# One core, attention fused with a rational-activation MLP: the iteration written as a table of 19 steps, one factor moved to another engine, sketches repeated by transfers

## The chip, the cores and the metric

The kernel runs on one core of a Trainium2 chip. The core has five engines that run their own queues of instructions in order and wait for each other on semaphores: PE (TensorE, matmuls; its weight loads are listed apart as PEld), DVE (VectorE), ACT (ScalarE), POOL (GpSimd) and SP (SyncE, which here only issues DMAs). The metric is the device time in microseconds. Three runs of the kernel before gave 311.78, 308.90 and 311.98 us, so the median is 311.78 us.

## The reference

Inputs are q, k and v of shape (4 batches, 4 heads, 1088 tokens, 32), two sketch matrices S1 and S2 of shape (8, 32), and the MLP's weights.

```python
def phi(x):                       # 64 features of a token
    a = einsum('rd,bhsd->bhsr', S1, x)
    b = einsum('rd,bhsd->bhsr', S2, x)
    return einsum('bhsi,bhsj->bhsij', a, b).reshape(..., 64)
q_p, k_p = phi(q), phi(k)
kv  = einsum('bhsf,bhsd->bhfd', k_p, v);  z = sum(k_p, axis=2)
x   = (q_p @ kv) / (q_p @ z + 1e-6)       # then 4352 tokens x 128
h   = x @ w_in                            # 4352 x 2048
P   = a[0] + a[1]*h + a[2]*h**2 + a[3]*h**3
Q   = 1 + |b[0]|*|h| + |b[1]|*h**2
out = (P / (Q + 1e-6)) @ w_out            # 4352 x 128
```

## The kernel before, in words

**The MLP, which is most of the work,** is cut into 34 units. Two units hold 256 tokens and half of the 2048 hidden columns each; the other 32 hold 512 tokens and a quarter of the hidden columns each. A unit's tile is always 128 x 2048 elements. Its steps are: `hidden` (PE, h = w_in·x in float32, in two halves), `evac` (ACT, copies each half from PSUM to the bf16 tile `hh`), `d_abs` (DVE, u = |h|), `d_w` (DVE, w = |b1|·u + |b0|), `d_y` (DVE, y = w·u), `a_ln` and `a_exp` (ACT, r = exp(-ln(1 + 1e-6 + y)) = 1/Q), `d_s` (DVE, s = h·r), `d_hs` (DVE, h·s), the linear factor p = a3·h + a2 (`d_p` on DVE in even units, `a_p` on ACT in odd units), `d_g` (DVE, g = p·hs), and `gather` (PE, which sums r, s and g against three scaled bf16 copies of w_out, w_out·a0, w_out·a1 and w_out, in four parts). `store` turns the finished block of outputs (DVE) and sends it out (SP).

**The attention** makes the columns of xT that `hidden` reads. Per batch, `Keys` (part 0 and part 1) has transposes (DVE), sketches (PE), copies of one sketch (ACT), features (DVE, the outer product), products with v (PE, over the whole sequence) and keep (ACT, writes the small matrix kvz). Per batch five blocks of `Queries` follow (four of 256 tokens and one of 64), each with transposes (DVE), sketches (PE), copies (ACT), features (DVE), products (PE), quotient (DVE: add 1e-6, reciprocal, multiply), back (PE transpose) and keep (ACT, into xT). In `Queries.sketches` a constant matrix `SAB` holds every sketch row eight times, so that four matmuls (two sketches for each of two pairs of heads, 64 rows deep, 128 columns out) write both factors of the outer product, already repeated, to PSUM. `copies` then brings one factor to SBUF in two ACT copies and `features` multiplies in two DVE instructions.

**What sets the order.** Nothing is reordered by a scheduler: each engine runs its instructions in the order in which the code is written. A loop runs over i from 0 to 37. Iteration i does evac and DVE's first three steps of unit i, `hidden` of unit i+1, `a_ln`, `a_exp` and `a_p` of unit i-1, `d_s`, `d_p`, `d_hs` and `d_g` of unit i-2, and `gather` of unit i-3. Between these steps the loop calls `gap()` five times; each call takes the attention stages that `plan` holds for that number of gap. A block of queries gets its eight stages in eight gaps one after another, beginning at gap 40·b - 31 + 7, 15, 22, 29 or 35. On DVE an iteration begins with `d_abs`, before `d_s` and `d_p`.

**The opening**, ahead of the loop, loads S1, S2, k and q of batch 0, w_in and w_out, and does the keys and the first two blocks of queries. `turn(n)` puts n matmuls on an idle tile between the steps (`TURNS = (12, 3, 0, 2, 2)`). The six scaled or plain copies of w_out (`w_part`) stand in gaps 4 to 9, that is in iterations 0 and 1.

**Buffers.** The pool `att` has three PSUM banks, `hps` two double banks for `hidden`, `ops` one bank for the output sum.

Of the kernel before, what the change touches and what calls it, by code (L numbers as in the profile page):

```python
# [18 lines left out]

@with_exitstack  # L20
def kernel(
# [149 lines left out]
    class Keys:  # L171
        def __init__(self, b, k_sb, v_sb, first=False):
            self.dst, self.k_sb, self.v_sb = kvz[b % 2], k_sb, v_sb
            self.take = wide if first else bank
# [13 lines left out]
        def sketches(self, part):  # L188
            t0, n = self.PARTS[part]
            ab = self.ab[part] = self.take()[:, 0:n * H * 2 * R].rearrange("p (t h s r) -> p t h s r", h=H, s=2, r=R)  # L190
            for t in range(t0, t0 + n):
# [1 line left out]
                nc.tensor.matmul(ab[:sl, t - t0].rearrange("p h s r -> p (h s r)"),
                                 lhsT=self.kT[:, t * 128:t * 128 + sl],
                                 rhs=S12.rearrange("p h s r -> p (h s r)"), start=True, stop=True)
# [4 lines left out]

        def copies(self, part):
            b_sk = self.b[part] = tmp.tile([128, 5, H, R], FP, name="b_sk")
            for ts, te, sl in self.spans(part):
                nc.scalar.copy(out=b_sk[:sl, ts:te], in_=self.ab[part][:sl, ts:te, :, 1, :])
# [34 lines left out]
    class Queries:  # L239
# [49 lines left out]

        def quotient(self):  # L290
            tl, T = self.tl, self.T
            nd = self.nd[:tl, 0:T * H * KW].rearrange("p (t h x) -> p (t h) x", t=T, h=H)
# [1 line left out]
            nc.vector.tensor_scalar(out=rec[:tl, :T * H], in0=nd[:, :, D], scalar1=1e-6, scalar2=None, op0=AX.add)
# [307 lines left out]
```

## Time and profile before

| | value |
|---|---|
| three runs, us | 311.78, 308.90, 311.98 |
| the profiled execution's own time | 310.26 us |
| its span | 308.5 us |
| mean granted TensorE clock | 0.977 |
| busy: PE, DVE, ACT | 284.8, 271.2, 244.4 us |
| share of the span: PE, DVE, ACT | 92%, 88%, 79% |
| DMA | 11.29 MB, 37 GB/s on the mean |

All positions below are microseconds from the start of the span. 1.76 us of the execution's own time lie outside the span. Four stages can be told apart: the opening (0 to 20.5, until the first `hidden`), the first four units (20.5 to 60.08, the last number being the start of unit 4's evac), the middle, in which batches 1 to 3 of the attention run between the units (60.08 to 245.84, the start of unit 27's evac), and the end without attention (245.84 to 308.5). The middle repeats itself: unit 4's evac starts at 60.08, unit 12's at 125.87, unit 20's at 191.66, so a round of eight units, with one batch of attention in it, takes 65.79 us. "A <- B" means that A waited for B, or, in the names of an instruction's tiles, that A is computed from B.

### The profile page before, as it was taken

To read this page: it belongs to the slowest core of one execution; us is meant where nothing else is said; L and a number is where in the kernel's file an instruction comes from. 1 tells how busy PE (TensorE), PEld (TensorE's weight loads), DVE (VectorE), ACT (ScalarE), POOL (GpSimd) and SP (SyncE) were. 2 spreads that over 40 slices of the span, in tenths; PEclk is the share of its full clock that TensorE was granted. 3 is DMA by queue.
4 is the path that set the end of the run, shared out by engine and by line. 5 is a ranking of instruction groups with operands and counts; after the bars stand their busy time and mean duration, and the time that the engine had idled before them with its cause. 6 is when DMAs were issued, how large, how long until landed. Compare 5 with 4: busy or idle time off the path is not lost.

```text
span 308.5 us, 3853 instructions
## 1 busy us (share of the span) xinstructions
PE 284.8 (92%) x1439; PEld 149.5 (48%) x1439; DVE 271.2 (88%) x383; ACT 244.4 (79%) x241; POOL 2.7 (1%) x22
## 2 busy tenths in 40 slices
PE   6999768999999999999999999999999998999392
PEld 2778445665455455545445554454454343434141
DVE  3526699899989999899999999899999999999992
ACT  1122858899888976898979778998889899999770
POOL 3000000000000000000000000000000000000000
PEclk9599979999999999999999999999999999999899
DMA  5990000002700200005500200010001000200102
GB/s 168 280 260 4 2 1 0 2 1 49 187 0 0 34 2 0 3 0 129 124 0 0 34 2 1 2 30 7 0 0 28 8 0 0 35 1 0 28 6 35
DMA packets 24626, 11.29 MB, mean 37 GB/s; under 512 B 20384, under 2 KB 22432, under 8 KB 24608
## 3 DMA queue, kind: packets, MB, share of 16 engines
q1 hardware_dynamic: 22976, 10.64, 14.5%
q10 hardware_dynamic: 1632, 0.41, 0.7%
q8 instruction: 11, 0.18, 0.2%
q14 instruction: 7, 0.06, 0.1%
HBM read 8.82 MB, written 2.23 MB: 36 GB/s over the span
## 4 chain that ended last, share of the span: by engine, by line
PE 46%; ACT 33%; DVE 15%; issue 3%; DMA 2%; SPq 0%; DVEq 0%; ACTq 0%
PE h_ps L337 21%; PE out_ps L408 10%; ACT r L376 9%; ACT p L368 8%; ACT hh L343 7%; ACT ln L372 6%; PE att_ps L260 4%; PE att_ps L226 3%; PE att_ps L286 3%; DVE hs L384 2%; DMA k_sb<-in_k_dram 2%; DVE s L380 2%; DVE g L388 2%; DVE y L356 1%; DVE w L352 1%
## 5 line engine op out<-in xcount | busy, mean ns | idle before, releaser
L337 PE MATMUL h_ps<-xT,w_in_sb 128*128 128x512 f32 (+1 forms) x288 | 130.6, 586 | 6.3 <-ACT hh L343 4.4
L337 PEld LDWEIGHTS h_ps<-xT,w_in_sb 128*128 128x128 f32 x288 | 51.7, 192 | 54.5 <-issue 38.7
L408 PEld LDWEIGHTS <-w_out 128*128 128x128 bf16 x420 | 40.5, 100 | 58.6 <-issue 26.6
L343 ACT CAST hh<-h_ps 128x1024 bf16<-128x1024 f32 x68 | 65.7, 1020 | 2.0 <-PE h_ps L337 2.0
L372 ACT ACTIVATE ln<-y 128x2048 f32<-128x2048 bf16 x34 | 65.6, 1930 | 1.9 <-DVE y L356 1.8
L376 ACT ACTIVATE r<-ln 128x2048 bf16<-128x2048 f32 x34 | 65.1, 1915 | 0.7
L408 PE MATMUL out_ps<-r,w_out 128*128 128x512 bf16 (+1 forms) x140 | 52.1, 372 | 5.3 <-DVE out_sb L419 5.3
L408 PE MATMUL out_ps<-g,w_out 128*128 128x512 bf16 (+1 forms) x140 | 52.1, 372 | 0.2 <-DVE g L388 0.2
L408 PE MATMUL out_ps<-s,w_out 128*128 128x512 bf16 (+1 forms) x140 | 52.0, 371 | 0.0
L388 DVE TENSOR_TENSOR g<-p,hs 128x2048 bf16<-128x2048 bf16 x34 | 41.2, 1213 | 0.2
L380 DVE TENSOR_TENSOR s<-hh,r 128x2048 bf16<-128x2048 bf16 x34 | 41.4, 1216 | 0.0
L356 DVE TENSOR_TENSOR y<-w,u 128x2048 bf16<-128x2048 bf16 x34 | 41.2, 1212 | 0.0
L384 DVE TENSOR_TENSOR hs<-hh,s 128x2048 bf16<-128x2048 bf16 x34 | 40.8, 1201 | 0.0
L368 ACT ACTIVATE p<-hh,a_sb 128x2048 bf16<-128x2048 bf16 x17 | 35.4, 2081 | 0.0
L347 DVE TENSOR_SCALAR u<-hh 128x2048 uint16<-128x2048 uint16 x34 | 23.3, 685 | 13.4 <-ACT hh L343 13.4
L352 DVE TENSOR_SCALAR w<-u,b_abs 128x2048 bf16<-128x2048 bf16 x34 | 27.4, 806 | 0.0
L286 PEld LDWEIGHTS att_ps<-kvz,q_pT 128*128 128x128 f32 (+1 forms) x144 | 18.0, 185 | 6.8 <-issue 3.3
L270 ACT COPY a_sk<-att_ps 128x256 f32<-128x256 f32 (+1 forms) x36 | 10.3, 342 | 10.9 <-PE att_ps L260 10.9
L260 PE MATMUL att_ps<-qT,SAB 64*128 64x256 f32 (+1 forms) x144 | 18.5, 376 | 0.0
L286 PE MATMUL att_ps<-kvz,q_pT 128*128 128x66 f32 (+1 forms) x144 | 18.1, 266 | 0.0
L308 ACT COPY xT<-att_ps 128x256 f32<-128x256 f32 (+1 forms) x20 | 6.8, 340 | 12.5 <-PE att_ps L303 12.5
L260 PEld LDWEIGHTS att_ps<-qT,SAB 64*128 64x128 f32 x144 | 11.7, 186 | 9.2 <-DVE u L347 4.5
(52 smaller groups left out, 160.8 us busy)
## 6 DMA issues: line engine op xcount, KB each, us to landing
k_sb<-in_k_dram SPq DMA_DIRECT2D x4, 544.0 KB, 4.8
v_sb<-in_v_dram SPq DMA_DIRECT2D x16, 128.0 KB, 5.2
q_sb<-in_q_dram SPq DMA_DIRECT2D x3, 544.0 KB, 6.3
out_dram<-out_sb SPq DMA_DIRECT2D x18, 64.0 KB, 2.0
w_in_sb<-in_moe_w_in_dram SPq DMA_DIRECT2D x4, 256.0 KB, 3.5
q_sb<-in_q_dram SPq DMA_DIRECT2D x1, 288.0 KB, 5.1
q_sb<-in_q_dram ACTq DMA_DIRECT2D x1, 256.0 KB, 3.2
out_dram<-out_sb SPq DMA_DIRECT2D x4, 56.0 KB, 1.9
```

The lines of the kernel that those rows point to most:

```text
L260: nc.tensor.matmul(self.sk[hp][:, i], lhsT=SAB[i][p, :], rhs=self.qT[p, :n], start=True, stop=True)
L286: nc.tensor.matmul(self.nd[:self.tl, o:o + 2 * KW], lhsT=self.q_p[:, c, t * self.tl:(t + 1) * self.tl], rhs=kvz[self.b % 2][:, c, :], star ...
L337: nc.tensor.matmul(t[:, x * tl:(x + 1) * tl], lhsT=w_in_sb[:, f * 128:(f + 1) * 128], rhs=xT[:, t0:t0 + tl], start=True, stop=True)
L343: nc.scalar.copy(out=live[i]["hh"][:, part * 1024:(part + 1) * 1024], in_=live[i]["h", part])
L356: nc.vector.tensor_mul(out=t, in0=live[i]["w"], in1=live[i]["u"])
L368: nc.scalar.activation(out=t, in_=live[i]["hh"], func=ACT.Identity, scale=a3, bias=a2)
L372: nc.scalar.activation(out=t, in_=live[i]["y"], func=ACT.Ln, bias=1.0 + 1e-6)
L376: nc.scalar.activation(out=t, in_=live[i]["ln"], func=ACT.Exp, scale=-1.0)
L380: nc.vector.tensor_mul(out=t, in0=live[i]["hh"], in1=live[i]["r"])
L384: nc.vector.tensor_mul(out=t, in0=live[i]["hh"], in1=live[i]["s"])
L388: nc.vector.tensor_mul(out=t, in0=live[i]["p"], in1=live[i]["hs"])
L408: nc.tensor.matmul(outs[t0][:, :tl], lhsT=w_sb[y][:, f, :], rhs=live[i][key][:, x * tl:(x + 1) * tl], start=(f == 0 and y == 0), stop=(f = ...
```

## The change

1. **A table of 19 steps.** `STEPS` lists an iteration as 19 steps, each with its lag to the unit. Attention stages can be put behind any single step (`K_SLOTS`, `Q_SLOTS` and so on are numbers of steps, 19 to an iteration), and no longer stand in neighbouring places: of the first block of queries, for example, the stages stand behind steps 46, 50, 52, 74, 78, 81, 84, 89 and 92. On DVE `d_s`, `d_p` and the turn of the outputs now come before `d_abs`.
2. **The linear factor** p is made on ACT in the units with i mod 8 in (1, 3, 4, 5, 7), and in the last eight units (26 to 33) in those with i mod 4 in (0, 1, 3). That is 22 units instead of 17.
3. **The queries of batches 1 to 3** (`Spread`) make each sketch value once: one matmul with the 128 x 64 matrix `S21`, one ACT copy of 64 rows to SBUF, two DMAs to a scratch tensor in DRAM (64 rows), and three DMAs back that read each row eight times, so that both factors lie repeated in SBUF. `features` is then one DVE multiplication from SBUF. All five DMAs are issued by SP. Batch 0 keeps the old form.
4. **The denominator.** Adding 1e-6 becomes a stage of its own (`plus`), on ACT; only the first two blocks of batch 0 keep it on DVE.
5. **Keys:** the last piece of the sequence is padded with zeros to 128, so copies and features take one instruction for each part instead of one or two.
6. **The opening:** the first half of q is loaded by SP, behind k, and not by ACT; there are 17 idle matmuls at the start, 2 between the two parts of the key sketches, 2 ahead of the first products and 2 at the end; five of the six `w_part` stand ahead of the loop, the sixth at step 28; the two halves of the first `hidden` come together, ahead of block B's products.

```diff
-    TURNS = (12, 3, 0, 2, 2)
+TURNS = (17, 2, 2, 2)
+STEPS = (("e0", 0), ("h0", -1), ("e1", 0), ("ln", 1), ("s", 2), ("pd", 2), ("st", 4), ("u", 0), ("h1", -1), ("g0", 3),
+    ("w", 0), ("ex", 1), ("pa", 1), ("hs", 2), ("g1", 3), ("y", 0), ("g2", 3), ("g3", 3), ("g", 2))
+P_ON_ACT = (1, 3, 4, 5, 7)
+P_LATE = (0, 1, 3)
...
-    nc.scalar.dma_start(out=q0[:, 0:512], in_=q0_src[:, 0:512])
+    nc.sync.dma_start(out=q0[:, 0:512], in_=q0_src[:, 0:512])
...
+        def plus(self):
...
+            else:
+                nc.scalar.activation(out=self.den[:tl, :T * H], in_=self.nv[:, :, D], func=ACT.Copy, bias=1e-6)
...
+    class Spread(Queries):
+        def sketches(self):
+            self.sk = bank()[0:2 * H * R, 0:self.n]
+            nc.tensor.matmul(self.sk, lhsT=S21.rearrange("p c s h r -> p (c s h r)"), rhs=self.qT[:, :self.n],
+                             start=True, stop=True)
+
+        def copies(self):
+            n, half = self.n, H * R
+            c = tmp.tile([2 * half, 256], FP, name="sk_sb")
+            nc.scalar.copy(out=c[:, :n], in_=self.sk)
+            d = dram.tile([half, 512], FP, name="sk_d")
+            for hp in range(2):
+                nc.sync.dma_start(out=d[:, hp * n:(hp + 1) * n], in_=c[hp * half:(hp + 1) * half, :n])
+            self.a, self.bb = (tmp.tile([128, 512], FP, name=x) for x in ("a_all", "b_all"))
+            nc.sync.dma_start(out=self.a[:, :2 * n],
+                              in_=bass.AP(tensor=d.tensor, offset=d.offset, ap=[[512, 2 * R], [0, R], [1, 2 * n]]))
+            for h2 in range(2):
+                nc.sync.dma_start(out=self.bb[h2 * 64:(h2 + 1) * 64, :2 * n],
+                                  in_=bass.AP(tensor=d.tensor, offset=d.offset + (2 + h2) * R * 512,
+                                              ap=[[0, R], [512, R], [1, 2 * n]]))
+
+        def features(self):
+            self.q_p = tmp.tile([128, 2, 256], FP, name="q_pT")
+            nc.vector.tensor_mul(out=self.q_p[:, :, :self.n], in0=self.a[:, :2 * self.n].rearrange("p (c n) -> p c n", c=2),
+                                 in1=self.bb[:, :2 * self.n].rearrange("p (c n) -> p c n", c=2))
...
+    def on_act(i):
+        return i % 8 in P_ON_ACT if i < NU - 8 else i % 4 in P_LATE
...
     for i in range(NU + 4):
-        if i < NU:
-            evac(i, 0)
...
+        for x, (name, lag) in enumerate(STEPS):
+            if 0 <= i - lag < NU:
+                does[name](i - lag)
+            for f in plan.pop(i * PER + x, ()):
+                f()
```

How the change moves instructions is shown at three places. The first is PE's queue in the middle, at a block of queries of batch 1 that lies inside a unit's `hidden` (`h_ps`); `qT` is the turned block, `SAB` the repeated sketch matrix, `kvz` the matrix from the keys. Before:

```order
L337 MATMUL h_ps<-xT,w_in_sb 128x512 x2
L260 MATMUL att_ps<-qT,SAB_146 128x256 x2
L260 MATMUL att_ps<-qT,SAB_148 128x256 x2
L337 MATMUL h_ps<-xT,w_in_sb 128x512 x2
L408 LDWEIGHTS w_out_151
```

And after, at the first place of this kind (`S_152` is S21):

```order
L384 MATMUL h_ps<-xT,w_in_sb 128x512 x2
L300 MATMUL att_ps<-kvz_133,q_pT 128x66 x4
L340 MATMUL att_ps<-qT,S_152 64x256
L384 MATMUL h_ps<-xT,w_in_sb 128x512 x2
L458 LDWEIGHTS w_out_160
```

Four matmuls of 256 columns have become one; it stands behind the products of the block before.

The second place is DVE's queue from the second block of queries (block B) of the opening to the first units. Before:

```order
L276 TENSOR_TENSOR q_pT<-h_ps,a_sk 128x512
L294 TENSOR_SCALAR rec<-att_ps 128x8
L295 RECIPROCAL rec<-rec 128x8
L297 TENSOR_TENSOR x_tok<-att_ps,rec 128x256
L247 STREAM_TRANSPOSE qT<-q_sb 128x256
L347 TENSOR_SCALAR u<-hh 128x2048
L352 TENSOR_SCALAR w<-u,b_abs 128x2048
```

And after (`w_out_160` to `w_out_162` are the three copies of w_out):

```order
L290 TENSOR_TENSOR q_pT<-h_ps,a_sk 128x512
L521 TENSOR_SCALAR w_out_160<-w_out_sb_f,a_sb 128x1024 x2
L521 TENSOR_SCALAR w_out_161<-w_out_sb_f,a_sb 128x1024
L261 STREAM_TRANSPOSE qT<-q_sb 128x256
L521 TENSOR_SCALAR w_out_161<-w_out_sb_f,a_sb 128x1024
L309 TENSOR_SCALAR den<-att_ps 128x8
L317 RECIPROCAL rec<-den 128x8
L319 TENSOR_TENSOR x_tok<-att_ps,rec 128x256
L523 CAST w_out_162<-w_out_sb_f 128x1024
L394 TENSOR_SCALAR u<-hh 128x2048
```

Five of the copies of w_out now stand ahead of the first `u`; before they stood between the steps of the first iterations.

The third place is ACT's queue in the middle, one unit with a block of queries. Before:

```order
L343 CAST hh<-h_ps 128x1024 x2
L372 ACTIVATE ln<-y 128x2048
L270 COPY a_sk<-att_ps 128x256 x2
L376 ACTIVATE r<-ln 128x2048
L343 CAST hh<-h_ps 128x1024 x2
```

And after (`den` is the new stage, `sk_sb` the copy of the 64 sketch rows):

```order
L390 CAST hh<-h_ps 128x1024 x2
L422 ACTIVATE ln<-y 128x2048
L312 ACTIVATE den<-att_ps 128x8
L426 ACTIVATE r<-ln 128x2048
L346 COPY sk_sb<-att_ps 64x256
L418 ACTIVATE p<-hh,a_sb 128x2048
L330 COPY xT<-att_ps 128x256
L390 CAST hh<-h_ps 128x1024 x2
```

The one copy of a sketch takes the place of two, `den` is new on this engine, and the copy stands at the end of the unit and not between `ln` and `r`.

More of the change, by code (lines that the diff above doesn't have):

```diff
@@ L133 @@
         nc.gpsimd.memset(t, 0.0)
+    kTs = [big.tile([128, (NT + 1) * 128], FP, name=f"kT{i}") for i in range(2)]
+    for t in kTs:
+        nc.gpsimd.memset(t[:, S:], 0.0)
     ident = consts.tile([128, 128], FP, name="ident")
@@ L364, in a_p @@
     def a_p(i):
-        if i % 2 == 0:
+        if not on_act(i):
             return
@@ L524, with place, once, get @@
-    slot = [0]
-    def gap():
-        for f in plan.pop(slot[0], ()):
-            f()
-        slot[0] += 1
+    for x, at in enumerate(W_SLOTS):
+        if at >= 0:
+            put(at, [lambda x=x: w_part(x)])
+    def place(obj, names, slots):
+        for n, at in zip(names, slots):
+            put(at, [lambda n=n: getattr(obj(), n[0])(*n[1:])])
+    def once(make):
+        box = []
+        def get():
+            if not box:
+                box.append(make())
+            return box[0]
+        return get
@@ new lines @@
+    Q_STAGES = [(n,) for n in ("transposes", "sketches", "copies", "features", "products", "plus", "quotient", "back",
+                               "keep")]
+    K_STAGES = [("transposes",), ("sketches", 0), ("copies", 0), ("sketches", 1), ("features", 0), ("copies", 1),
+                ("products", 0), ("features", 1), ("products", 1), ("keep",)]
+    place(lambda: QC, Q_STAGES[2:-1], QC_SLOTS)
+    place(once(lambda: Queries(0, q0, cuts[3], cuts[4])), Q_STAGES, QD_SLOTS)
+    place(once(lambda: Queries(0, q0, cuts[4], cuts[5])), Q_STAGES, QE_SLOTS)
@@ L531 @@
+    for b in range(1, B):
+        at = 8 * PER * (b - 1)
+        put(max(at - 15, 0), [lambda b=b: fetch(b)])
+        place(once(lambda b=b: Keys(b, fetched[b][0], fetched[b][1])), K_STAGES, [at + x for x in K_SLOTS])
+        for y in range(5):
+            place(once(lambda b=b, y=y: Spread(b, fetched[b][2], cuts[y], cuts[y + 1])), Q_STAGES,
+                  [at + x for x in Q_SLOTS[y]])
     hidden(0, 0)
+    hidden(0, 1)
+    for x in range(3):
+        w_part(x)
     QB.products()
+    QC.transposes()
@@ L533 @@
+    QC.sketches()
+    w_part(3)
+    QB.plus()
     QB.quotient()
[L534 to L570 removed]
+    w_part(4)
@@ new lines, in hide, with fill @@
+    def hide(i, part):
+        if i == 2 and part == 0:
+            QC.keep()
+        hidden(i, part)
+    def fill(i, part):
+        evac(i, part)
+        if i == 0 and part == 1:
+            QB.back()
+            QB.keep()
+    does = {"e0": lambda i: fill(i, 0), "e1": lambda i: fill(i, 1), "h0": lambda i: hide(i, 0),
+            "h1": lambda i: hide(i, 1), "u": d_abs, "w": d_w, "y": d_y, "ln": a_ln, "ex": a_exp, "pa": a_p, "pd": d_p,
+            "s": d_s, "hs": d_hs, "g": d_g, "g0": lambda i: gather(i, 0), "g1": lambda i: gather(i, 1),
+            "g2": lambda i: gather(i, 2), "g3": lambda i: gather(i, 3), "st": store}
```

133 lines of the change are left out of this document (41 added, 92 removed).

## The prediction

> **What bounds the kernel now.** I began with the busy times by stage, because the shares of the whole span (PE 92%, DVE 88%) mix four stages with different limits. In this view a row gives from:to, its length, the busy time of each engine with its count of instructions, the granted TensorE clock, the DMA share and GB/s.
>
> ```profile
> 0.00:20.50 20.50, 17.38 (x135) 10.90 (x135) 7.75 (x18) 4.10 (x12) 2.72 (x22) 0.83 0.85 238
> 20.50:60.08 39.58, 33.95 (x225) 23.13 (x226) 31.26 (x54) 25.00 (x36) 0.00 (x0) 0.96 0.06 16
> 60.08:245.84 185.76, 183.41 (x912) 94.42 (x911) 177.39 (x257) 164.59 (x162) 0.00 (x0) 1.00 0.12 27
> 245.84:308.50 62.66, 50.03 (x171) 21.09 (x169) 54.77 (x57) 50.68 (x35) 0.00 (x0) 0.97 0.08 13
> ```
>
> The middle (60.08 to 245.84) is 60% of the span, and there PE is busy for 183.4 of 185.8 us and DVE for 177.4. One round of eight units in it, and the waits in the same 65.79 us (who waited for whom, us in total, times, longest):
>
> ```profile
> 125.87:191.66 65.79, 64.88 (x336) 33.29 (x335) 63.02 (x91) 57.35 (x60) 0.00 (x0) 1.00 0.15 34
> ACT xT L308 <- PE att_ps L303: 3.0, 3, 1.2
> DVE u L347 <- ACT hh L343: 2.4, 3, 1.4
> ACT kvz L235 <- PE att_ps L226: 2.4, 1, 2.4
> ACT a_sk L270 <- PE att_ps L260: 2.0, 3, 0.8
> ACT b_sk L204 <- PE att_ps L193: 0.8, 1, 0.8
> ```
>
> PE has 0.9 us of a round to spare, DVE 2.8, ACT 8.4. ACT's spare time is nearly all waiting for attention steps of PE (3.0 + 2.4 + 2.0 + 0.8 = 8.2 us); nearly all of DVE's spare time is `u` waiting for evac. So in the middle PE is the bound, with DVE close behind. The end is ACT's:
>
> ```profile
> 245.84:285.28 39.44, 37.43 (x123) 16.09 (x122) 38.33 (x41) 39.25 (x28) 0.00 (x0) 1.00 0.05 7
> ```
>
> In the opening and the first four units no engine is full: there the chain from step to step sets the time.
>
> **The opening.** The rows are stretches of the timeline and of the chain that ended last (start, length), and three windows, the third for the key sketches (line 193) of a later batch alone.
>
> ```profile
> 1.19 4.17 PE L119 MATMUL out_ps<-idle 128*128 128x512 bf16 x12 [1.19 <-DVE idle L114]
> 7.16 3.83 PE h_ps L193 x18
> 10.99 1.39 PE out_ps L119 x3
> 12.38 2.01 PE h_ps L260 x8
> 18.48 1.09 PE h_ps L260 x8
> 5.40:7.10 1.70, 0.00 (x0) 0.00 (x0) 0.70 (x2) 0.00 (x0) 0.00 (x0) 1.00 0.69 185
> 8.00:14.00 6.00, 6.00 (x26) 4.15 (x25) 3.27 (x5) 0.60 (x3) 0.00 (x0) 0.50 0.94 276
> 110.20:114.20 4.00, 2.34 (x18) 2.21 (x18) 1.00 0.00 0
> ```
>
> Twelve idle matmuls end at 5.36; PE then stands until k has come and been turned (7.16), and from 8 to 14 its clock is granted at 0.50. The key sketches take 3.83 us there against 2.34 at clock 1.00, and the first query sketches 2.01 against 1.09. Seventeen idle matmuls at 4.17/12 = 0.35 us end at 1.19 + 5.9 = 7.1, just when the sketches can start. If it is the gap that costs the clock, 1.5 + 0.9 us go; of the three idle matmuls (1.39 us at half clock) two remain at about 0.25 each, -0.9. That is -3.3. DVE's two key features, which follow the sketches, cannot move up by all of it, so I take **-3.0** (0 if the clock falls anyway, -4.2 if k also comes earlier, as q no longer leaves beside it). Against it, with q on SP the loads of v, w_in and w_out go out one place later in that queue; of these v comes first, and its products wait for the features anyway, which covers it.
>
> [...]
>
> **The first four units.** The copies of w_out leave this stage. Their row, three of PE's waits there, and DVE's two largest up to 57.6 us:
>
> ```profile
> L471 DVE TENSOR_SCALAR w_out<-w_out_sb_f,a_sb 128x1024 bf16<-128x1024 f32 x4 | 2.9, 746 | 0.0
> 33.88 3.70 PE L337 MATMUL h_ps<-xT,w_in_sb 128*128 128x512 f32 x8 [1.53 <-ACT xT L308]
> 39.67 0.44 PE L303 MATMUL att_ps<-ident,x_tok 128*128 128x128 f32 x2 [1.25 <-DVE x_tok L297]
> 42.03 3.45 PE L337 MATMUL h_ps<-xT,w_in_sb 128*128 128x512 f32 x4 [1.33 <-ACT hh L343]
> DVE rec L294 <- PE att_ps L286: 6.3, 4, 2.8
> DVE u L347 <- ACT hh L343: 4.4, 2, 2.3
> ```
>
> The four scaled copies alone are 2.9 us of DVE in the chain that ends in x_tok, xT and hh. Five of six now stand ahead of the first `u`, around the early `rec`, where DVE waits anyway (6.3 and 4.4 us). PE has 39.58 - 33.95 = 5.6 us of waiting in this stage, which bounds the gain. The three waits quoted sum to 4.1; the attention stages still hand on from engine to engine and the reordered `d_s`, `d_p` matter only from unit 0's `s` on, so I take **-3.0**, with -1.0 and -5.6 as bounds.
>
> **The middle, engine by engine, for a round of eight units.**
>
> ```profile
> 136.75 1.06 PE att_ps L260 x8
> 234.40 0.59 PE att_ps L260 x8
> 20.51 1.99 PE h_ps L337 x8
> L362 DVE TENSOR_SCALAR p<-hh,a_sb 128x2048 bf16<-128x2048 bf16 x4 | 3.2, 805 | 0.0
> L294 DVE TENSOR_SCALAR rec<-att_ps 128x8 f32<-128x8 f32 x4 | 0.6, 159 | 0.0
> L368 ACT ACTIVATE p<-hh,a_sb 128x2048 bf16<-128x2048 bf16 x4 | 8.3, 2081 | 0.0
> L270 ACT COPY a_sk<-att_ps 128x256 f32<-128x256 f32 x9 | 2.9, 374 | 2.0 <-PE att_ps L260 2.0
> L235 ACT COPY kvz<-att_ps 64x33 f32<-64x33 f32 x4 | 0.7, 181 | 2.4 <-PE att_ps L226 2.4
> ```
>
> - PE: four sketch matmuls with their weight loads take 1.06 us (0.59 for the block of 64 tokens). They are 64 rows deep and overlap in pairs, so one matmul is not a quarter of that. The nearest row for one float32 matmul of 256 columns with its weights is line 337's four pairs in 1.99: 0.50. So -0.56 for each of four blocks and about -0.4 for the small one (its new cost lies between 0.12, a quarter of 0.50, and 0.50; I take 0.2): -2.6. Keys' padding adds under 0.1. PE: 64.9 - 2.6 = 62.3.
> - DVE: one p less, -0.8; five additions of 1e-6 at 0.16, -0.8; the merged features at most -0.3. DVE: 63.0 - 1.9 = 61.1.
> - ACT: one p more, +2.1; `den` five times, nearest row the 64x33 copy at 0.18, +0.9; one sketch copy of 0.37 less for each of four blocks, and about 0.2 for the small one, -1.7. ACT: 57.35 + 1.3 = 58.6.
>
> With `u` behind `d_s` and `d_p`, DVE has work while evac runs, which is where its 2.4 us went; what is late next is PE again. PE at 62.3, with the 0.9 us of waits that it has now, gives 63.2 a round, -2.6. The stage holds 185.76/65.79 = 2.82 rounds: **-7.3 us**. Bounds: 0, if every wait only changes its name; DVE alone at 61.1, -4.7 a round, -13.2.
>
> What must stay hidden is the way through DRAM.
>
> ```profile
> 72.81 1.82 SPq L427 DMA_DIRECT2D out_dram<-out_sb  x4
> out_dram<-out_sb SPq DMA_DIRECT2D x18, 64.0 KB, 2.0
> q_sb<-in_q_dram ACTq DMA_DIRECT2D x1, 256.0 KB, 3.2
> q_sb<-in_q_dram SPq DMA_DIRECT2D x3, 544.0 KB, 6.3
> ```
>
> An issue on SP takes 1.82/4 = 0.45 us; a store lands 2.0 us after its issue. Two writes: 0.45 + 2.0 = 2.45. Three reads (256, 128 and 128 KB): the third issue begins 0.9 later and lands 3.2 after it if it is like the 256 KB row, 6.3 if like the 544 KB row: 6.5 or 9.7 us in all, and I take the first, since the middle's DMA share is 0.12. From `copies` to `features` the table leaves 21 or 22 steps of 19, from late in one unit's queue on ACT to late in the next unit's on DVE, so about one unit: 63.2/8 = 7.9 us. That covers 6.5. Behind an SP that waits for a copy or a write stand only stores, later blocks and loads for the next batch, which are issued two units and more ahead of their first use.
>
> **The end.** ACT is full, so the extra p counts; these are the last waits:
>
> ```profile
> 292.73 1.91 ACT L372 ACTIVATE ln<-y 128x2048 f32<-128x2048 bf16 x1 [1.79 <-DVE y L356]
> 294.82 0.81 DVE L362 TENSOR_SCALAR p<-hh,a_sb 128x2048 bf16<-128x2048 bf16 x1
> ```
>
> Unit 28's p adds 2.0. Unit 32's falls into the 1.79 us in which ACT waits for y (+0.2), and takes 0.8 from DVE's last chain. Sum **+1.4**; if ACT comes to the end ahead, -0.8, and +4 if both p count in full and DVE's 0.8 is hidden.
>
> **Sum.** -3.0 - 3.0 - 7.3 + 1.4 = -11.9 on the profiled execution's 310.26 us: 298.4. The median of the three runs is 1.5 above that execution and their lowest 1.4 below it, so I add nothing for this and keep 1.5 either way.
>
> **Rivals.**
> - B, the sketches come too late. DVE waits in `features` of twelve large blocks. At 9.7 us against 7.9 each is 1.8 late, 21.6 us, of which DVE's spare 2.1 a round (63.2 - 61.1) takes 5.9: 298.4 + 15.7 = 314, slower. It costs more than the whole gain from (11.9 + 5.9)/12 = 1.5 us of lateness, a chain of 9.4. For it: 6.3 is a measured landing, and the loads of the next batch share the queue. Against: they meet one block in five.
> - C, ACT becomes the bound and keeps its 8.2 us of waits: 58.6 + 8.2 = 66.8 a round, +1.0 times 2.82, so 310.26 - 3.0 - 3.0 + 2.8 + 1.4 = 308.5. Against: in the new order `keep` and `copies` stand several steps behind what they wait for.
> - D, the clock falls as before: 298.4 + 3.0 = 301.4.
> - E, everything hides: -4.2 - 5.6 - 13.2 and nothing at the end: 287.
> - That one part does nothing is inside the bounds: no part is needed by another.
>
> **How the numbers follow.** Forecast 0.60 (its own range 293 to 304), D 0.13, C 0.11, B 0.08, E 0.08. A measurement of this kernel tells about 1% from no change, 3.1 us, so faster means below 308.7. Forecast, D, E and 0.04 of C lie there: 0.85; the other 0.07 of C is "same"; B, 0.08, is slower. The range 291 to 308 leaves out B, half of E and about 0.06 of the forecast's tails.
>
> **What would show it.** Right: PE's clock at 1.00 through the key sketches, the first `hidden` near 17.5, unit 4's evac near 54, a round of about 63.2 with `u` no longer waiting, and ACT's waits for attention below 5 us a round. Wrong: DVE waiting for a DMA in `features` (B); ACT busy with waits above 66 (C); clock 0.50 near 8 us (D). The forecast as a whole is wrong if the round stays above 65.

## The result and the profile after

| | before | after |
|---|---|---|
| median, us | 310.53 (308.90 to 311.98, 4 runs) | 300.81 (299.67 to 301.90, 4 runs) |
| profiled execution, us | 310.26 | 299.67 |
| its span, us | 308.5 | 297.9 |
| ratio of the times | | 0.9695, 95% interval 0.9649 to 0.9742 |

The changed kernel is 3.1% faster by the medians. The medians here and below are over all runs of a kernel; the ratios leave out runs in a slower state of the chip, more than 1.5% above the fastest of the same kernel. Its profiled execution is 10.6 us below that of before; the forecast was 11.9.

The first view of the changed kernel is busy time by stage: from:to, length, busy time of PE, PEld, DVE, ACT and POOL with their counts, granted clock, DMA share, GB/s. The first row is the opening and a little more. The next three are the first four units, the middle and the end, cut at the same events as before (the first `hidden`, the starts of the evacs of units 4 and 27). The last two are two rounds of eight units.

```profile
0.00:18.10 18.10, 15.93 (x140) 9.94 (x141) 7.66 (x17) 4.11 (x11) 3.15 (x26) 1.00 0.83 221
17.81:53.69 35.88, 32.07 (x222) 22.55 (x223) 29.63 (x49) 24.77 (x36) 0.00 (x0) 1.00 0.28 62
53.69:235.09 181.40, 177.24 (x826) 88.46 (x824) 173.18 (x223) 167.39 (x163) 0.00 (x0) 1.00 0.28 65
235.09:297.90 62.81, 48.77 (x171) 20.57 (x169) 54.65 (x55) 54.45 (x37) 0.00 (x0) 0.98 0.09 13
53.69:117.73 64.04, 61.99 (x319) 32.18 (x317) 60.16 (x78) 58.18 (x58) 0.00 (x0) 1.00 0.31 72
117.73:181.25 63.52, 62.44 (x307) 31.30 (x306) 61.38 (x79) 58.09 (x59) 0.00 (x0) 1.00 0.30 75
```

Stage by stage against before: the first `hidden` at 17.81 rather than 20.51 us (-2.7), the first four units 35.88 rather than 39.57 (-3.7), the middle 181.40 rather than 185.76 (-4.4), the end 62.81 rather than 62.66 (+0.15). The sum is -10.6.

In the middle PE has 177.2 us of work where it had 183.4: the work fell by 6.2 us, the stage by 4.4, so PE now stands 4.2 us there and not 2.4. ACT's work rose from 164.6 to 167.4. The gain lies in the two rounds (64.04 and 63.52 us, before 65.79 each). What is left of the middle, units 20 to 26, hardly changed; before, and then after:

```profile
191.66:245.84 54.18, 53.59 (x223) 26.18 (x222) 51.41 (x76) 49.88 (x46) 0.00 (x0) 1.00 0.06 11
181.25:235.09 53.84, 52.81 (x204) 24.98 (x203) 51.63 (x68) 51.12 (x47) 0.00 (x0) 1.00 0.19 46
```

The opening in the timeline of PE (start, length, operation, count, idle time before it and what ended that):

```profile
1.19 5.93 PE L132 MATMUL out_ps<-idle 128*128 128x512 bf16 x17 [1.19 <-DVE idle L127]
7.67 1.10 PE L212 MATMUL h_ps<-S,kT 128*128 128x64 f32 x8 [0.55 <-DVE kT L203]
10.56 1.14 PE L274 MATMUL h_ps<-qT,SAB 64*128 64x256 f32 x8 [0.29 <-DVE k_p L224]
```

The seventeen idle matmuls end at 7.12 and PE then stands 0.55 us. The clock stays at 1.00, and the first query sketches take 1.14 us where they took 2.01. The key sketches begin at 7.67 rather than 7.16: k came later (DVE waits 3.1 us for it, before 2.4).

The waits in the two rounds (who waited for whom, total us, times, longest). The lines ahead of the dots are from the first round, the others from the second:

```profile
DVE q_pT L360 <- DMA b_all<-sk_d: 2.2, 1, 2.2
ACT den L312 <- PE att_ps L300: 1.8, 3, 0.9
...
ACT den L312 <- PE att_ps L300: 2.0, 3, 1.4
ACT xT L330 <- PE att_ps L325: 1.6, 2, 1.2
DVE q_pT L360 <- DMA b_all<-sk_d: 0.5, 1, 0.5
```

In these rounds DVE no longer waits in `u`. ACT's waits for attention are 3.6 us in the second round (8.2 before). New is a wait of DVE for the way through DRAM, 2.2 us in the first round for one block of queries. The two passes that came late look like this on ACT, SP and DVE:

```profile
81.34 0.36 ACT L346 COPY sk_sb<-att_ps 64x256 f32<-64x256 f32 x1
81.73 1.73 SPq L349 DMA_DIRECT2D sk_d<-sk_sb  x2
85.98 0.54 SPq L351 DMA_DIRECT2D a_all<-sk_d  x1
86.57 1.22 SPq L354 DMA_DIRECT2D b_all<-sk_d  x2
90.78 0.69 DVE L360 TENSOR_TENSOR q_pT<-a_all,b_all 128x512 f32<-128x512 f32 x1 [2.18 <-DMA b_all<-sk_d]
...
146.57 0.36 ACT L346 COPY sk_sb<-att_ps 64x256 f32<-64x256 f32 x1
146.96 0.79 SPq L349 DMA_DIRECT2D sk_d<-sk_sb  x2
149.05 0.54 SPq L351 DMA_DIRECT2D a_all<-sk_d  x1
149.63 1.22 SPq L354 DMA_DIRECT2D b_all<-sk_d  x2
154.30 0.69 DVE L360 TENSOR_TENSOR q_pT<-a_all,b_all 128x512 f32<-128x512 f32 x1 [0.47 <-DMA b_all<-sk_d]
```

From the end of the copy to the features: 154.30 - 146.93 = 7.4 us in the second pass. In the first it is 90.78 - 81.70 = 9.1 us, with 4.25 us from the first write's issue to the first read's instead of 2.1. The load of the next batch's q had gone out 3.6 us ahead of the first write in the first pass (at 78.12) and 4.6 us ahead in the second (at 142.34). My estimate had been 6.5, and 9.7 at worst. A third block waited 0.56 us (217.89); by then no batch is left to load.

### The profile page after: what moved, and what is told of

It is laid out like the page before. It is cut to its first block, busy times and chain, and to the rows that moved or that the text cites. A ratio compares the mean times of both kernels' runs of the same rounds, so it can differ in the third digit from the quotient of the medians.

```text
span 297.9 us, 3779 instructions
## 1 busy us (share of the span) xinstructions
PE 273.7 (92%) x1353; PEld 141.2 (47%) x1353; DVE 264.8 (89%) x341; ACT 250.7 (84%) x245; POOL 3.1 (1%) x26
## 4 chain that ended last, share of the span: by engine, by line
PE 46%; ACT 25%; DVE 14%; DMA 8%; issue 3%; SPq 2%; DVEq 0%; ACTq 0%
PE h_ps L384 23%; PE out_ps L458 14%; ACT r L426 7%; ACT hh L390 6%; ACT ln L422 6%; ACT p L418 5%; DMA w_out_sb_f<-in_moe_w_out_dram 3%; PE att_ps L300 3%; DVE hs L434 3%; DMA b_all<-sk_d 2%; DMA v_sb<-in_v_dram 2%; DVE g L438 2%; PE att_ps L240 2%; DVE y L403 2%; DVE s L430 1%
## 5 line engine op out<-in xcount | busy, mean ns | idle before, releaser
L384 PE MATMUL h_ps<-xT,w_in_sb 128*128 128x512 f32 (+1 forms) x288 | 129.3, 583 | 9.4 <-ACT hh L390 7.7
L384 PEld LDWEIGHTS h_ps<-xT,w_in_sb 128*128 128x128 f32 x288 | 50.8, 189 | 58.0 <-issue 37.6
L458 PE MATMUL out_ps<-g,w_out 128*128 128x512 bf16 (+1 forms) x140 | 51.3, 367 | 2.6 <-DVE g L438 2.6
L458 PE MATMUL out_ps<-r,w_out 128*128 128x512 bf16 (+1 forms) x140 | 51.4, 367 | 2.4 <-DVE out_sb L469 2.4
L458 PE MATMUL out_ps<-s,w_out 128*128 128x512 bf16 (+1 forms) x140 | 51.3, 367 | 0.0
L418 ACT ACTIVATE p<-hh,a_sb 128x2048 bf16<-128x2048 bf16 x22 | 45.9, 2086 | 0.0
L434 DVE TENSOR_TENSOR hs<-hh,s 128x2048 bf16<-128x2048 bf16 x34 | 41.4, 1217 | 0.1
L360 DVE TENSOR_TENSOR q_pT<-a_all,b_all 128x512 f32<-128x512 f32 (+1 forms) x15 | 9.1, 605 | 3.3 <-DMA b_all<-sk_d 3.2
L240 PE MATMUL att_ps<-v_sb,k_p 128*64 128x64 f32 (+1 forms) x288 | 11.0, 225 | 0.6 <-ACT sk_sb L346 0.6
L240 PEld LDWEIGHTS att_ps<-v_sb,k_p 128*64 128x64 f32 (+1 forms) x288 | 9.6, 137 | 3.2 <-issue 2.0
```

The lines of the kernel that those rows point to most:

```text
L384: nc.tensor.matmul(t[:, x * tl:(x + 1) * tl], lhsT=w_in_sb[:, f * 128:(f + 1) * 128], rhs=xT[:, t0:t0 + tl], start=True, stop=True)
L418: nc.scalar.activation(out=t, in_=live[i]["hh"], func=ACT.Identity, scale=a3, bias=a2)
L434: nc.vector.tensor_mul(out=t, in0=live[i]["hh"], in1=live[i]["s"])
L458: nc.tensor.matmul(outs[t0][:, :tl], lhsT=w_sb[y][:, f, :], rhs=live[i][key][:, x * tl:(x + 1) * tl], start=(f == 0 and y == 0), stop=(f = ...
```

## Experiments

The first question was which parts of the change carry the gain, the second why the middle fell short. The ratio to the kernel before, which was measured again beside each group of experiments (medians 310.26 to 311.87 us), stands behind each time, with its interval. A trace is of one execution, so a difference of a microsecond in a single stage rests on one execution a side. The changed kernel itself has 300.81 us, 0.9695 (0.9649 to 0.9742).

**1. The opening's idle matmuls.** Twelve as before the change, not seventeen.

```diff
-TURNS = (17, 2, 2, 2)
+TURNS = (12, 2, 2, 2)
```

> The kernel after with 12 idle matmuls at the start and not 17; nothing else changes. If the gap on PE costs the clock (forecast): PE idles from about 5.4 to 7.6, the granted clock falls to 0.50 for some 6 us, and the first hidden comes near 20.5 and not at 17.81; the whole is 2.5 to 3 us longer than the kernel after (about 303). [...]

Measured: 303.83 us, 0.9779 (0.9716 to 0.9841). The timeline of PE in this run, and then the window from 8 to 14 us:

```profile
1.19 5.27 PE L132 MATMUL out_ps<-idle 128*128 128x512 bf16 x12 [1.19 <-DVE idle L127]
7.77 1.10 PE L212 MATMUL h_ps<-S,kT 128*128 128x64 f32 x8 [1.32 <-DVE kT L203]
```

```profile
8.00:14.00 6.00, 6.00 (x50) 4.92 (x51) 4.42 (x7) 1.14 (x3) 0.00 (x0) 0.64 1.05 280
```

With five idle matmuls fewer PE stands 1.32 us, the clock falls (0.64 on the mean of these 6 us), and the first `hidden` comes at 20.62 rather than 17.81. The gap costs the clock, and the clock costs 2.8 us.

**2. Without the transfers.** All batches make their sketches in the old form; sketches and copies stand later, behind the places of the old chain, so that the PSUM banks suffice. Everything else is as changed.

```diff
-            place(once(lambda b=b, y=y: Spread(b, ...
+            place(once(lambda b=b, y=y: Queries(b, ...
```

> The kernel after, with the old four-matmul sketches for the queries of all batches (sketches and copies stand later, 3 to 11 steps ahead of features, since they hold PSUM banks until then). If PE's load carries the middle: PE's busy time in a round goes from 62.4 back to about 65, the round from 63.5 to 65.5 or 66, the whole to about 306. If the rounds are held by ACT or DVE instead, the round grows by less than 1 us and the whole stays below 303.

Measured: 306.76 us, 0.9887 (0.9851 to 0.9924). The first four units and the middle of this run:

```profile
17.75:54.97 37.22, 32.33 (x225) 22.57 (x226) 30.09 (x50) 25.04 (x37) 0.00 (x0) 1.00 0.18 41
54.97:242.57 187.60, 182.68 (x899) 95.20 (x911) 175.19 (x237) 170.97 (x179) 0.00 (x0) 1.00 0.13 26
```

The middle is 6.2 us longer than in the changed kernel and 1.8 longer than before the change. So the new order, p on ACT and den on ACT bring the middle nothing without the transfers, at least with the old sketches at these places, which are not those of before.

**3. The transfers alone.** The kernel before with only this part of the change. Transposes, sketches and copies move forward so that the copies stand seven gaps ahead of the features.

```diff
-                    box2["q"] = Queries(b, fetched[b][2], cuts[x], cuts[x + 1])
+                    box2["q"] = Spread(b, fetched[b][2], cuts[x], cuts[x + 1])
...
+            names = ("transposes", "sketches", "copies", "features", "products", "quotient", "back", "keep")
+            for n, d in zip(names, (-6, -5, -4, 3, 4, 5, 6, 7)):
+                put(at + lag + d, [later(Q, n)])
```

> The kernel before, with the repeated sketches through DRAM in batches 1 to 3 alone (transposes to copies six gaps earlier, the rest in place). PE's busy time in a round falls by 2.6. If PE held the rounds: 65.8 to about 63.5 or 64, the whole 4 to 6 us shorter than before (305 to 306). If DVE, at 63.0 with its waits for evac, holds them as closely: 65, the whole 1 to 2 us shorter.

Measured: 305.12 us, 0.9823 (0.9755 to 0.9890). Its first four units and its middle:

```profile
17.17:55.69 38.52, 33.56 (x218) 22.69 (x219) 30.31 (x54) 24.86 (x35) 0.00 (x0) 0.96 0.23 57
55.69:237.52 181.83, 176.82 (x816) 87.51 (x828) 176.94 (x242) 162.36 (x147) 0.00 (x0) 1.00 0.28 65
```

The middle is 181.83, within half a microsecond of the changed kernel's. With the transfers alone the middle gains as much as with the whole change. In the two rounds DVE has no wait of 0.5 us or more for a transfer, but over the run it waits again 9.0 us for evac in `u`. The profiled execution (301.63 us) is the fastest of the four runs: its first `hidden` came at 17.17, since the clock stayed up in its opening (1.00 from 1.45 to 18.52 us; last section).

**4. `u` ahead of `s`.** Only this step of the table goes back.

```diff
-STEPS = (..., ("ln", 1), ("s", 2), ("pd", 2), ("st", 4), ("u", 0), ("h1", -1), ...
+STEPS = (..., ("ln", 1), ("u", 0), ("s", 2), ("pd", 2), ("st", 4), ("h1", -1), ...
```

> The kernel after, with DVE's u ahead of s and p in each iteration, as before the change. If the new place of u is what took away DVE's waits for evac: DVE waits 2 us or more a round for evac again, rounds 1 to 2 us longer, the whole 303 to 305. If PE alone holds the rounds: DVE waits, but the rounds and the whole stay within 1 us.

Measured: 303.95 us, 0.9791 (0.9745 to 0.9837), about 3 us more than changed. Middle and end by windows, and then one row of PE's timeline:

```profile
54.72:237.84 183.12, 176.78 (x813) 88.41 (x824) 172.64 (x223) 167.28 (x163) 0.00 (x0) 1.00 0.28 65
237.84:302.00 64.16, 50.86 (x168) 21.29 (x169) 54.07 (x55) 54.45 (x37) 0.00 (x0) 0.93 0.09 13
```

```profile
283.61 0.59 PE L458 MATMUL out_ps<-r,w_out 128*128 128x512 bf16 x1 [4.20 <-DVE out_sb L469]
```

`u` waits again, 1.0 and 1.3 us in the two rounds, but the middle's 183.12 lies inside what kernels with the same middle show (181.40 to 183.55, experiment 8). The end is 1.35 us longer: PE stands 4.20 us until DVE has turned the outputs, and in the two stretches from 282.30 to 285.71 and on to 289.13 the clock is at 0.51 and 0.50. Another 0.9 us is in the first four units (36.81). So the place of `u` counts, mostly at the edges and not in the middle, where I had put it.

**5. The copies of w_out back in the loop.**

```diff
-W_SLOTS = (-1, -1, -1, -1, -1, 28)
+W_SLOTS = (10, 15, 18, 28, 30, 35)
```

> The kernel after, with the six copies of w_out inside the loop (behind steps 10, 15, 18, 28, 30 and 35) and none ahead of it. In the kernel after DVE stands 2.2 us for w_out's load with the copies ahead of the first u. If that wait is on the path: unit 0's u comes about 2 us earlier and unit 4's evac 1 to 2 us earlier than 53.7; the whole 298.5 to 300. If the copies cost more inside the loop than the wait ahead of it (the reason given in the prediction for a gain of 3 us): unit 4's evac 1 to 3 us later, the whole 302 to 304.

Measured: 300.80 us, 0.9714 (0.9680 to 0.9748), the same as changed. The first four units take 35.51 us (35.88 changed). The 3.7 us of this stage do not come from the copies of w_out.

**6. The linear factor as before the change** (ACT in odd units only).

```diff
-P_ON_ACT = (1, 3, 4, 5, 7)
-P_LATE = (0, 1, 3)
+P_ON_ACT = (1, 3, 5, 7)
+P_LATE = (1, 3)
```

> The kernel after, with p on ACT in the odd units alone (17 and not 22), as before the change. ACT has 2.1 us a round less, DVE 0.8 more. If PE and DVE hold the rounds (forecast): rounds 63.5 to 64.2, the end about 2 us shorter up to the last ln and up to 2 longer behind it, the whole 299 to 301. If ACT holds the rounds by now: rounds about 62, the whole near 295.

Measured: 298.35 us, 0.9634 (0.9587 to 0.9680). ACT's 5 units of 8 are no gain; by the medians this version is 2.5 us better, though the two intervals still overlap. Its profiled execution (300.45 us) is the slowest of the four; in it the clock fell once in the first four units:

```profile
18.65:55.99 37.34, 33.78 (x222) 23.23 (x223) 29.65 (x49) 24.78 (x37) 0.00 (x0) 0.95 0.23 58
```

Its middle took 180.89 and its end 61.82 us.

**7. Unit 28 alone.** Its p goes back to DVE.

```diff
-        return i % 8 in P_ON_ACT if i < NU - 8 else i % 4 in P_LATE
+        return i % 8 in P_ON_ACT if i < NU - 8 else i in (27, 29, 31, 32, 33)
```

> The kernel after, with unit 28's p on DVE and not on ACT (unit 32's stays on ACT). If ACT alone holds the end: 2.0 us less from unit 27's evac to the last ln (48.9 to 46.9), the whole 1 to 2 us shorter. If DVE is as full there: DVE's 0.7 us come on, and the whole changes by less than 0.7.

Measured: 300.08 us, 0.9671 (0.9619 to 0.9723), no difference in the time. In the trace the end shrinks from 62.81 to 61.48 us, and the middle of this execution is longer by about as much (182.96):

```profile
236.32:297.80 61.48, 49.83 (x168) 21.10 (x169) 55.22 (x57) 52.50 (x36) 0.00 (x0) 0.97 0.09 13
```

**8. Less time for the transfers.** The features of twelve blocks stand five steps earlier.

```diff
-Q_SLOTS = ((46, 50, 52, 74, ...), (79, 81, 87, 108, ...), (97, 105, 112, 134, ...), (130, 132, 138, 160, ...
+Q_SLOTS = ((46, 50, 52, 69, ...), (79, 81, 87, 103, ...), (97, 105, 112, 129, ...), (130, 132, 138, 155, ...
```

> The kernel after, with features of the twelve large repeated blocks five steps earlier, so that the way through DRAM (7.5 us measured from the copy's end to the landing) no longer fits. Rival B's price: DVE waits for a DMA in each, 1 to 2.5 us, some 20 us in all; with DVE 2 us from full a round, the whole is 8 to 16 us longer than the kernel after (309 to 317). If such waits are taken up by slack: less than 3 us longer.

Measured: 309.25 us, 0.9959 (0.9924 to 0.9994): 8.4 us lost, nearly the whole gain. The list of DVE's waits over the whole run of this kernel and its middle:

```profile
DVE q_pT L360 <- DMA b_all<-sk_d: 14.4, 7, 4.1
```

```profile
53.99:243.83 189.84, 177.73 (x813) 88.17 (x824) 174.47 (x222) 168.31 (x164) 0.00 (x0) 1.00 0.26 62
```

Three other kernels have the changed kernel's middle unaltered: those of experiments 1, 5 and 7. The same two rows of them, in this order:

```profile
DVE q_pT L360 <- DMA b_all<-sk_d: 5.5, 3, 2.5
```

```profile
55.93:239.48 183.55, 177.04 (x813) 88.44 (x824) 172.98 (x223) 167.59 (x164) 0.00 (x0) 1.00 0.28 65
```

Experiment 5:

```profile
DVE q_pT L360 <- DMA b_all<-sk_d: 3.4, 3, 2.0
```

```profile
53.25:234.94 181.69, 176.49 (x813) 88.48 (x824) 173.37 (x223) 167.49 (x164) 0.00 (x0) 1.00 0.28 65
```

Experiment 7:

```profile
DVE q_pT L360 <- DMA b_all<-sk_d: 4.8, 3, 3.0
```

```profile
53.36:236.32 182.96, 176.54 (x813) 88.47 (x824) 173.07 (x223) 167.48 (x163) 0.00 (x0) 1.00 0.28 65
```

With the changed kernel (3.2 us waited in all, middle 181.40) these are four executions of the same middle. Ordered by the wait, 3.2, 3.4, 4.8 and 5.5 us go with 181.40, 181.69, 182.96 and 183.55: each microsecond waited is about 0.94 of the middle. Drawn on to no wait this gives 181.40 - 0.94 x 3.2 = 178.4. Of the 14.4 us in this experiment 13.2 lie in the middle (the first wait, 1.23 us, ends ahead of it), which by that line would give 190.8; it measured 189.84. So a late transfer is paid almost in full, and DVE's spare time does not absorb it.

By parts it is clearer. The same four executions, with the length of each part and DVE's wait for transfers in it (one block each), in us:

| | first round | waited | second round | waited | units 20 to 26 | waited |
|---|---|---|---|---|---|---|
| before | 65.79 | | 65.79 | | 54.18 | |
| changed | 64.04 | 2.18 | 63.52 | 0.47 | 53.84 | 0.56 |
| experiment 1 | 64.35 | 2.50 | 65.35 | 2.31 | 53.85 | 0.67 |
| experiment 5 | 62.80 | 0.95 | 65.04 | 2.00 | 53.85 | 0.44 |
| experiment 7 | 64.86 | 3.01 | 64.26 | 1.22 | 53.84 | 0.59 |

Less the wait, the first round takes 61.85 or 61.86 us in all four and the second 63.04 or 63.05: in the rounds each microsecond of lateness costs one. Units 20 to 26 take the same time whatever the wait, so something else holds them.

**9. More time for the transfers.** Transposes, sketches and copies of the first four blocks of each later batch stand four steps earlier.

```diff
-Q_SLOTS = ((46, 50, 52, 74, ...), (79, 81, 87, 108, ...), (97, 105, 112, 134, ...), (130, 132, 138, 160, ...
+Q_SLOTS = ((42, 46, 48, 74, ...), (75, 77, 83, 108, ...), (93, 101, 108, 134, ...), (126, 128, 134, 160, ...
```

> Transposes, sketches and copies of the first four query blocks of each later batch stand four steps earlier, so that the way through DRAM has about 1.7 us more (4/19 of a round's eighth, 8.0 us); the features stay where they were. In the profiled execution of the changed kernel DVE waited 3.2 us for these transfers (2.2 us in the first round), in its relatives 3.4 to 5.5 us, and features put five steps earlier cost 8.5 us. Theory 'these waits still cost': they go, the middle falls from 181.4 to about 179, the time to about 298.5. Rival 'they fill DVE's spare time': the waits go, the middle stays within 1 us, the time stays at 300 to 301.5.

Measured: 307.51 us, 0.9916 (0.9874 to 0.9958). That is 6.7 us slower than changed; neither theory holds. The first four units and the middle by windows, and then two of the waits:

```profile
18.22:58.27 40.05, 34.81 (x207) 23.55 (x208) 30.03 (x49) 24.89 (x36) 0.00 (x0) 0.87 0.22 52
58.27:243.89 185.62, 177.54 (x826) 89.18 (x838) 173.99 (x223) 167.66 (x164) 0.00 (x0) 1.00 0.28 64
```

```profile
DVE rec L317 <- ACT den L312: 11.2, 13, 2.6
ACT sk_sb L346 <- PE att_ps L340: 6.8, 3, 2.6
```

DVE's wait for the transfers is gone. In its place stand others: ACT waits 6.8 us for the sketches at the head of its queue (no such wait in the changed kernel), and DVE 11.2 us for `den` (3.0 changed). In the first four units the clock falls twice (0.50 from 31.56 to 34.97 and from 48.63 to 55.45 us). An earlier step is a different neighbour in three queues, and here that cost more than the 1.7 us of lead were worth. What the middle would be with the waits for DRAM gone and nothing put in their place therefore stays open; 178.4 is a line through four executions, not a measurement.

**10 and 11. The same with ACT relieved.** Both have the lead of experiment 9, p on ACT in units 1, 3, 5 and 7 of eight, and in the end in units 27, 29, 31, 32 and 33; the second also has den on DVE.

```diff
-            if self.first:
+            if True:
                 nc.vector.tensor_scalar(out=self.den...
```

> The lead of four steps, ScalarE with the linear factor in units 1, 3, 5 and 7 of eight (as before the change), and in the end in units 27, 29, 31, 32 and 33 (unit 28 left out). Theory 'ScalarE was given one unit too many': about 1 us less in the middle, 1.3 in the end (62.8 to 61.5), with the lead's 2: 296. Rival 'the gain of the run with odd units was chance': no faster than the run with the lead alone.

> As the run before, with the addition of 1e-6 back on VectorE: ScalarE has 5 x 0.18 = 0.9 us less a round, VectorE 0.8 more and no wait for den (1.0 us a round). Theory 'ScalarE's load sets the middle': a little faster, by up to 0.9 x 2.8 = 2.5 us. Rival 'PE sets it and both are covered': within 1 us of the run before.

Measured: 306.26 us, 0.9872 (0.9835 to 0.9909), and 304.85 us, 0.9853 (0.9814 to 0.9892). The lead spoils both: their middles are 185.89 and 184.78 us. The ends are 61.15 and 61.57 rather than 62.81. By their times, whose intervals overlap, these two do not tell whether den belongs on ACT. In units 20 to 26 the second is shorter, 53.32 us against 54.26.

**12. ACT relieved, without the lead.** The changed kernel with its own places, and the two moves of 10 and 11.

> The changed kernel with its own places for the sketches, ScalarE's linear factor in units 1, 3, 5 and 7 of eight and, in the end, 27, 29, 31, 32 and 33, and the addition of 1e-6 on VectorE in all blocks. Against the run with odd units alone (298.35) unit 32's factor is on ScalarE, where it fell into a wait for y of 1.3 us (-0.5), and den is on VectorE (the pair of runs with the lead: -1.4, at the edge of what they tell). Theory 'work given to ScalarE beyond the sketch copies it lost only costs': 296.5 to 298, below the changed kernel's 300.8. Rival 'the two moves to ScalarE are neutral': 300 to 301.

Measured: 298.27 us, with a kernel before of 311.87 us beside it: 0.9559 (0.9500 to 0.9617). The interval lies wholly below the changed kernel's, and five of its six runs (297.36 to 299.60) are below the changed kernel's fastest (299.67), so this version beats both kernels. Against experiment 6 (0.9587 to 0.9680) it cannot be told apart. Its middle and its end:

```profile
53.15:233.98 180.83, 175.83 (x826) 88.64 (x824) 176.79 (x240) 160.90 (x145) 0.00 (x0) 1.00 0.29 66
233.98:295.60 61.62, 49.87 (x171) 21.00 (x169) 55.39 (x57) 52.58 (x36) 0.00 (x0) 0.96 0.09 13
```

ACT has 6.5 us less work in the middle than in the changed kernel and DVE 3.6 more; the middle is 0.6 shorter and the end 1.2. So what was handed to ACT was not needed. In the middle this kernel differs from experiment 6 by den alone, and its units 20 to 26 take 53.11 us against 53.85.

## Why the prediction was right or wrong

The time, 300.81 against 298.4, lies inside the forecast's own range, and of the signs that I had named all but one came: clock 1.00 through the sketches, first `hidden` at 17.81 (17.5), unit 4's evac at 53.69 (54), no `u` waiting in the rounds, ACT's attention waits at 3.6 us in the second. The round of 63.2 came out at 64.04 and 63.52. That the sum came within 1.3 us (-11.9 against -10.6) is in part luck: the middle came 2.9 us short, and the first four units and the end came 0.7 and 1.25 us better than forecast, for other causes than those that I had named.

**The opening: right, with its cause.** Forecast -3.0, measured -2.7; experiment 1 gives it back when the gap returns. The better end (k earlier, as q no longer leaves beside it) was wrong in sign: the sketches began 0.5 us later. In the kernel before, in which ACT loads q, DVE waits 2.4 us for k; with q on SP it waits 3.1 us in the changed kernel and 2.9 to 4.9 in experiments 1, 5, 7 to 10 and 12. The move alone was not tried, so the cause stays open. Rival D would have the clock fall anyway. It did not (1.00 from 0 to 18.10 us), but it was nearer than I thought: the gap's length alone did not decide, since 1.32 us cost the clock in experiment 1 and 2.28 us did not in experiment 10 (below).

**The first four units: right in size, wrong in cause.** Forecast -3.0 for the copies of w_out, measured -3.7, and their place makes no difference (experiment 5). I had taken DVE's work in a chain for a price without asking whether the same copies elsewhere would hit another wait: ahead of the loop DVE waits 2.2 us for w_out to arrive. Three other things were taken out one by one. Without the transfers the stage is 1.3 us longer, with `u` first 0.9. The third is the clock: it fell once in this stage before the change (from 41.6 to 45.0) and not after it. In experiment 6, where it also fell once, the stage took 37.34 us, 1.5 more than changed. Together that is 3.7, but that the three add up was not tried.

**The middle: right mechanism, too large.** Forecast -7.3, measured -4.4, and between -2.2 and -4.4 in the four executions of the same middle. The engines' work was sized well: PE 62.0 and 62.4 a round (forecast 62.3), DVE 60.2 and 61.4 (61.1), ACT 58.2 and 58.1 (58.6). Two steps failed, and rounds that were better than forecast in all else hid part of it.

The first is "PE at 62.3, with the 0.9 us of waits that it has now": PE stood 2.0 and 1.1 us in the two rounds. Beside it stands the estimate of 6.5 us for the way through DRAM against a cover of 7.9: it measured 7.4, and 9.1 in the first round. So rival B came true for three blocks of the later batches at 1 us on the mean, and in the two rounds its 2.65 us were paid in full (table of experiment 8). Rival B's other number, that DVE's spare time absorbs the first 5.9 us, is refuted by the same table. In the other direction, the rounds less these waits are 61.86 and 63.05, on the mean 0.75 below the 63.2 of the forecast.

The second is "The stage holds 185.76/65.79 = 2.82 rounds": it took 0.82 of a round's gain, 2.1 us, for units 20 to 26, where 0.3 came. In all four executions of the same middle they take 53.84 or 53.85 us, so late transfers are not the reason. Experiments 6 and 12, and 10 and 11, differ in the middle by den alone, and with den on DVE this part is 0.7 and 0.9 us shorter; what holds the rest is not known. So the middle fell short by 2.65 (late transfers) - 1.5 (rounds better than forecast) + 1.8 (units 20 to 26) = 2.95, the forecast's 7.3 less 4.4. The line of experiment 8 gives 0.94 x 3.2 = 3.0 for the waits, nearly the same number, but that is a coincidence.

That `u` moves and p goes to ACT I had counted into this stage as needed. Experiment 2 shows that the gain needs the transfers, experiment 3 that they alone bring as much, and experiment 6 that the fifth p on ACT is not needed. Whether the new order adds anything is open: experiment 3 has rounds of 64.03 and 64.31 us without a wait of 0.5 us or more for a transfer, the changed kernel 61.86 and 63.05 less its waits, so the new order may have gained what its own late transfers took back.

**The end: too high.** Forecast +1.4, measured +0.15. Up to ACT's last `ln` the 2.0 us for unit 28's p came as forecast: from unit 27's evac to that `ln` it is 48.88 us (235.09 to 283.97), before it was 46.89, and in experiment 7, without this p on ACT, it is 46.94. The mis-sized term is the last chain, for which I had +0.2 - 0.8: from the last `ln` to the end of the span it is now 13.9 us, before it was 308.5 - 292.73 = 15.8, so 1.9 less. In the traces DVE's last `s` now starts 3.86 us behind that `ln` (at 287.83) and waits 0.60 us for ACT's r; before, it came 5.28 us behind (at 298.01), since DVE still had unit 32's `s`, p, `hs` and g to do. That this nearly cancels the 2.0 is luck.

**Rivals C and E.** ACT has 58 us of work a round and far fewer waits, so C did not happen in the middle. Still, relieving ACT gains about 1% (experiment 12), half of it at the end. E had the end at nothing and everything else at its best; only the end came near.

## What to carry to other kernels

Work that a bottleneck engine no longer does is worth its busy time only if its replacement arrives in time: price the whole replacement chain (here 7.4 us in one pass and 9.1 in another) against its cover, and count each late microsecond in full where all engines are above 90%, as in these rounds. Compare a stage by its parts over several executions: a sum can agree by chance where the parts do not. Then test each part alone. Here one part was enough for the middle's gain, one for the opening's, and the work moved to another engine, which looked like balance, cost time. In queues without reordering a place is good for its neighbours, so moving a step "a little earlier" to gain slack can cost more than the wait it removes (6.7 us against 3.2 in experiment 9).

## What the runs showed of the hardware that I had not expected

**The falls and rises of the granted clock lie on a grid of about 3.41 us.** In the trace of before they are at 7.47, 14.30, 41.60, 45.02, 290.78, 294.19 and 307.84 us. From 7.47 to 294.19 it is 286.72 us, which is 84 times 3.413; in units of that from the first, the seven are at 0, 2.0, 10.0, 11.0, 83.0, 84.0 and 88.0. In the ten other traces with more than one edge the edges also lie on multiples: cut at these into windows, every whole window has a clock of 0.50 or 0.51, or of 0.99 or 1.00. The start of the grid differs from execution to execution: its first line in the span is at 0.84 us in experiment 9, at 2.10 in experiment 10 and at 2.32 in experiment 11. Below are pairs of neighbouring windows of that grid (length, then PE's busy time; the clock is the third number from the right). Before the change:

```profile
4.06:7.47 3.41, 1.60 (x9) 0.70 (x7) 1.07 (x2) 0.23 (x1) 0.23 (x1) 1.00 0.81 234
7.47:10.89 3.42, 3.42 (x18) 3.21 (x16) 1.91 (x4) 0.27 (x1) 0.00 (x0) 0.50 1.00 261
```

With twelve idle matmuls (experiment 1):

```profile
6.29:9.70 3.41, 2.09 (x17) 1.78 (x16) 2.36 (x5) 0.27 (x1) 0.00 (x0) 1.00 1.12 231
9.70:13.11 3.41, 3.41 (x21) 2.47 (x21) 2.58 (x3) 0.48 (x2) 0.00 (x0) 0.50 1.03 298
```

Experiment 10, in the opening:

```profile
5.51:8.93 3.42, 1.65 (x8) 0.56 (x6) 0.25 (x1) 0.00 (x0) 0.00 (x0) 1.00 1.06 291
8.93:12.34 3.41, 2.69 (x22) 2.44 (x23) 2.73 (x5) 0.53 (x2) 0.00 (x0) 1.00 0.90 226
```

Experiment 6, in the first four units:

```profile
28.91:32.32 3.41, 1.90 (x15) 1.17 (x14) 1.83 (x5) 2.08 (x6) 0.00 (x0) 1.00 0.00 0
32.32:35.73 3.41, 3.41 (x4) 1.50 (x5) 2.14 (x4) 2.65 (x2) 0.00 (x0) 0.50 0.02 5
```

A window in which PE stood 1.81, 1.32 or 1.51 us was followed by one at half clock, and one in which it stood 1.77 us was not. Over the traces of this case every window at full clock with more than 2.0 us of standing was followed by a fall (two windows that end less than 0.5 us ahead of the span's end left out) and none with less than 1.3; between them both occur, so that something besides PE's idle time counts, which the runs do not tell. A fall lasts one window or two: the opening's lasted two in the traces of before and of experiment 1, although PE stood 0.00 us in them. So the length of a gap does not decide alone: ahead of the key sketches PE stood 2.28 us in experiment 10 (7.16 to 9.44), the grid cut this in two (1.77 us of standing in one window, 0.72 in the next), and the clock stayed up; 1.32 us in experiment 1 lay inside one window and cost 2.8. The kernel with the transfers alone, with the twelve idle matmuls of before, stood 1.22 us in its profiled execution (in the window from 4.87 to 8.28), and it kept its clock (1.00 in the next).
